# Attention before a mixture of experts: the softmax guard and the factor 8 carried by a 121st row of the matmuls

## The chip, the core and the metric

The kernel runs on one core of one Trainium2 chip, as one launch. The metric is the device time of that launch in microseconds (us). The core has five engines with a queue each: PE (TensorE, matrix products), DVE (VectorE), ACT (ScalarE), POOL (GpSimd) and SP (SyncE, which here issues transfers). An engine takes its instructions in order, so an instruction that waits holds back everything behind it on that engine. SBUF is the on-chip memory of 128 partitions, PSUM the memory that PE writes.

## The reference

```python
k_p = k.reshape(B, H, Sp, pool, D).mean(axis=3)      # B, H, S, D = 8, 8, 576, 64; pool = 8, Sp = 72
v_p = v.reshape(B, H, Sp, pool, D).mean(axis=3)
scores = scale * np.matmul(q, k_p.transpose(0, 1, 3, 2))
scores = scores - np.max(scores, axis=-1, keepdims=True)
attn = np.exp(scores)
attn = attn / (np.sum(attn, axis=-1, keepdims=True) + 1e-09)
attn_out = np.matmul(attn, v_p)
...
x = attn_out.transpose(0, 2, 1, 3).reshape(B, S, H * D)
# each token: an expert e (its best, or that of the token before, by a local gate), then
out[b, s] = p[e] * (np.maximum(x[b, s] @ w1[e], 0.0) @ w2[e])
```

The `1e-09` in the fourth line from the attention's end is the guard that this case is about. The factor 8 is the pool: the kernel sums eight values where the reference takes their mean.

## The kernel before

The attention is cut into 20 units (`units`): four pairs of batches by five, the first four of a pair with 128 partitions of queries in two columns, the fifth (`stacked`) with the last 64 queries of both batches. All eight heads of a batch have 8 x 72 = 576 keys in a row, and these are cut into five pieces of `KC` = 120 keys (`VB` holds where each begins). A piece covers parts of two or three heads; `VCH` lists them, and there are 11 such (piece, head) columns in all.

For a unit, PE makes the scores (L504, L510), DVE takes the maxima (`mx`, L525) and subtracts them (`ap`, L528), ACT takes exp (L538), PE transposes pieces of 120 keys (L554) and ACT copies them into `aT` (L401). Then PE multiplies `aT[0:120]` with `vaug` (L585). `vaug` holds for each of the 11 columns a mask times the pooled values (64 numbers), the mask itself, and 9 numbers for routing: so one product gives the output, the softmax sum and the routing numbers. ACT copies the product to `osb` (L401). `scale` then makes the reciprocal of the sums on DVE in two instructions:

```python
nc.vector.tensor_scalar(out=rr[:, 0:ns], in0=osb[:, 0:ns, HD], scalar1=EPS, scalar2=float(POOL), op0=ALU.add, op1=ALU.mult)
nc.vector.reciprocal(out=rr[:, 0:ns], in_=rr[:, 0:ns])
```

These are L602 and L603. `rr` then scales the routing numbers (`lgx`, L607) and the rows (`xs`, L623, on POOL and DVE).

The masks `mk` are made once by `mask_consts` (L204 to L220): POOL sets a table, DVE turns it into 0 and 1 in small instructions (L212 to L216) and copies it into the four `vaug` buffers (L220). `prep_k` loads keys (`kk`), DVE adds them eight by eight into `kd` (L428, one buffer) and ACT spreads that into `kdz` (L432). `prep_v` loads values, pools them into `vs` (L416 on DVE, L409 to L411 on POOL), PE transposes them (L456), ACT copies them to `vT`, and PE multiplies with the gate (L465, L468).

The order of all this is a list written out by hand: `PLAN` holds steps as `name:number`, and `do` issues them in that order on whichever engine each uses. `cm` is `mask_consts`, `cr` is `route_consts` (small constants on POOL, L223 to L251, used much later), `cz` clears a `kdz` buffer on POOL (L817), `fr` is the step with L602 and L603, `wa` are products that only keep PE at work. After `PLAN`, `PLAN_B` and `PLAN_C` begin the expert layers, which share the queues with the last units; then a loop over blocks of 256 tokens runs (from L1252).

Of the kernel before, what the change touches and what calls it, by code (L numbers as in the profile page):

```python
# [16 lines left out]
P = 128  # L17
# [90 lines left out]
def moe_attention(ctx: ExitStack, tc: tile.TileContext, q, q_st, k, v, v_st, w_gate, w1, w2, out):  # L108
# [95 lines left out]
    def mask_consts():  # L204
        nc.gpsimd.iota(prow_i, pattern=[[0, 1]], base=0, channel_multiplier=1)
        nc.vector.tensor_copy(out=prow, in_=prow_i)
        nc.vector.tensor_scalar(out=bm[:, 1:2], in0=prow, scalar1=float(HP), scalar2=None, op0=ALU.is_ge)
        nc.vector.tensor_scalar(out=bm[:, 0:1], in0=prow, scalar1=float(HP), scalar2=None, op0=ALU.is_lt)
        for c, hs in enumerate(VCH):
            for i, h in enumerate(hs):  # L210
                nc.gpsimd.memset(mkt[:, VOFF[c] + i:VOFF[c] + i + 1], float(VB[c] - G * h))
        nc.vector.tensor_scalar(out=mkt, in0=mkt, scalar1=prow[:, 0:1], scalar2=None, op0=ALU.add)  # L212
        nc.vector.tensor_scalar(out=mk, in0=mkt, scalar1=0.0, scalar2=None, op0=ALU.is_ge)
        nc.vector.tensor_scalar(out=mkt, in0=mkt, scalar1=float(G), scalar2=None, op0=ALU.is_lt)
        nc.vector.tensor_tensor(out=mk, in0=mk, in1=mkt, op=ALU.mult)
        nc.vector.scalar_tensor_tensor(out=mk[:, VOFF[4]:VOFF[4] + 1], in0=prow, scalar=float(4 * KC - VB[4]),  # L216
                                       in1=mk[:, VOFF[4]:VOFF[4] + 1], op0=ALU.is_ge, op1=ALU.mult)

        for t in vaug:
            nc.vector.tensor_copy(out=t[:, :, HD], in_=mk)  # L220

    def route_consts():
        nc.gpsimd.affine_select(out=lt, in_=ones, pattern=[[1, P]], compare_op=ALU.is_gt, fill=0.0,  # L223
# [160 lines left out]
    with ExitStack() as actx:  # L384
# [57 lines left out]
        def prep_v(bb, cc):  # L442
            vt = vaug[bb % NBUF]
            m = 2 if cc < 2 else 1
            vt_in = buffer([P, 2, D], "vt_in")
            if m == 2:
                nc.sync.dma_start(vt_in.rearrange("p c n -> p (c n)"), v[bb, cc])
            else:
                nc.sync.dma_start(vt_in[:, 0], v_st[bb])
            yield  # L450
            vs = pooled_v[bb, cc] = ap2.tile([P, 2, HD], F32, name="vs", bufs=5)
            pooled(vs[0:KC, 0:m], vt_in[0:KC, 0:m], KC, m, {"d": 2, "s": 1}.get(pick["e"], 0))
            yield
            tp = ps_t.tile([P, 512], F32, name="tp")
            busy(tp, TFILL.get((bb, cc), 0))
            nc.tensor.transpose(out=tp[0:m * HD, 0:KC], in_=vs[0:KC, 0:m].rearrange("p c d -> p (c d)"), identity=ident[0:KC, 0:KC])  # L456
            yield
            vT = ap2.tile([P, P], F32, name="vT")
            copy(vT[0:m * HD, 0:KC], tp[0:m * HD, 0:KC])
            yield  # L460
            mp = ps_r.tile([P, 512], F32, name="rt")
            busy(mp, GFILL.get((bb, cc), 0))
            if m == 2:
                w = wg[:, 0:162] if cc == 0 else wg[:, 27:207]
                nc.tensor.matmul(out=mp[0:KC, 0:54].rearrange("p (c x) -> p c x", c=2), lhsT=vT[:, 0:KC],  # L465
                                 rhs=w.rearrange("p (c x) -> p c x", c=2)[:, :, 0:27], start=True, stop=True)
            else:
                nc.tensor.matmul(out=mp[0:KC, 0:2 * GL], lhsT=vT[0:HD, 0:KC], rhs=wg[0:HD, (H - 2) * GL:H * GL], start=True, stop=True)  # L468
            yield
            for ci in range(m):  # L470
                c = 2 * cc + ci
                o, ns = VOFF[c], len(VCH[c])
                nc.vector.tensor_tensor(out=vt[0:KC, o:o + ns, HD + 1:SEG],
                                        in0=mp[0:KC, 27 * ci:27 * ci + ns * GL].rearrange("p (h e) -> p h e", e=GL),
                                        in1=mk[0:KC, o:o + ns].unsqueeze(2).broadcast_to([KC, ns, GL]), op=ALU.mult)

        def place_v(bb, cc):
            vt, vs = vaug[bb % NBUF], pooled_v[bb, cc]
            for ci in range(2 if cc < 2 else 1):
                c = 2 * cc + ci  # L480
                o, ns = VOFF[c], len(VCH[c])
                if pick["e"] == "a":
                    for i in range(o, o + ns):
                        nc.scalar.activation(out=vt[0:KC, i, 0:HD], in_=vs[0:KC, ci, :], func=AF.Copy, scale=mk[0:KC, i:i + 1])
                    continue
                (nc.vector if pick["e"] == "d" else nc.gpsimd).tensor_tensor(
                    out=vt[0:KC, o:o + ns, 0:HD], in0=vs[0:KC, ci:ci + 1, :].broadcast_to([KC, ns, HD]),
                    in1=mk[0:KC, o:o + ns].unsqueeze(2).broadcast_to([KC, ns, HD]), op=ALU.mult)

        def queries(i):  # L490
            pr, t = units[i]
# [49 lines left out]
        class Attend:  # L541
            def __init__(self, at, pr, t):
                self.at, self.pr, self.t = at, pr, t
                self.stacked = t == 4
                self.aT = ap2.tile([P, NCH, P], F32, name="aT")

            def transpose(self, c4):
                cs = list(range(4 * c4, min(4 * c4 + 4, len(VB) if self.stacked else NCH)))
# [9 lines left out]
            def values(self, g):  # L558
# [7 lines left out]
                def heads(n, r, c0, c, lo, hi, at):  # L566
                    hs = [h for h in VCH[c] if lo <= h < hi]
                    if hs:
                        at += (hs[0] - lo) * SEG
                        o = VOFF[c] + VCH[c].index(hs[0])  # L570
                        jobs.append((n, op[r, at:at + len(hs) * SEG], self.aT[0:KC, c0 + c, r],
                                     vaug[(2 * self.pr + n) % NBUF][0:KC, o:o + len(hs), :].rearrange("p s x -> p (s x)")))
                if self.stacked:
                    lo, hi = ((0, HM), (HM, H))[g]
                    for c in range(len(VB)):
# [21 lines left out]
            def scale(self, lg):  # L597
# [196 lines left out]
        def do(name, n):  # L794
# [515 lines left out]
```

## Time and profile before

| what | value |
|---|---|
| three timed runs, median (lowest to highest) | 606.49 us (604.74 to 607.5) |
| the profiled execution: its time, its span | 610.27 us, 607.8 us |
| mean granted TensorE clock in the span | 0.992 |
| instructions in the span | 14315 |

The span runs from the first to the last instruction, so 2.47 us of the profiled execution lie outside it. [...] Durations below come from this one execution.

### The profile page before, as it was taken

Reading aid. Unit: us, or ns where it says so; the run is one execution under the profiler, and the core shown is the slowest. Engines: PE = TensorE matmul, PEld = TensorE weight load, DVE = VectorE, ACT = ScalarE, POOL = GpSimd, SP = SyncE. Lnnn points to the kernel's source line nnn. Section 1 sums busy time; section 2 is a strip of 40 time slices with the busy share of each in tenths; the row PEclk is TensorE's granted clock in tenths of the full one; section 3 lists DMA queues with packets and bytes.
Section 4 is the critical chain, followed back from the end, with each engine's and each line's share of the span. In section 5 each row is a group of like instructions: output and inputs, shape, how many; then the busy total and the mean of one; then the engine's idle time right before and its main releaser. Section 6 shows DMA issues by size and latency. Waiting matters only on the chain.

```text
span 607.8 us, 14315 instructions
## 1 busy us (share of the span) xinstructions
PE 580.0 (95%) x3316; PEld 500.3 (82%) x3317; DVE 410.0 (67%) x981; ACT 318.0 (52%) x708; POOL 283.2 (47%) x527
## 2 busy tenths in 40 slices
PE   8999998898999999999999999999999999999991
PEld 7998988796877878888888888888888888888981
DVE  7999899899857424652883585798536586525680
ACT  2778777886523223442752474667344374433561
POOL 6686786777682335233143426154252333331352
PEclk9999999999999999999999999999999999999996
DMA  8998984965103764322483467496733276223223
GB/s 347 406 354 294 361 301 114 336 164 191 36 2 104 253 218 135 109 104 69 155 312 94 142 182 296 128 339 202 294 119 114 104 228 221 104 69 121 87 74 88
DMA packets 62274, 111.96 MB, mean 184 GB/s; under 512 B 13730, under 2 KB 34210, under 8 KB 62244
## 3 DMA queue, kind: packets, MB, share of 16 engines
q1 hardware_dynamic: 53732, 89.54, 44.0%
q0 software_dynamic: 8512, 22.07, 10.5%
q8 instruction: 13, 0.21, 0.1%
q14 instruction: 17, 0.14, 0.1%
HBM read 81.88 MB, written 31.80 MB: 187 GB/s over the span
## 4 chain that ended last, share of the span: by engine, by line
PE 82%; DVE 9%; POOL 2%; issue 2%; DMA 2%; ACT 1%; POOLq 0%; DVEq 0%; ACTq 0%
PE o_ps L380 35%; PE hp L353 14%; PE hp L355 7%; PE tp L353 5%; PE hp L1006 5%; PE op L585 4%; PE sp L504 3%; PE rt L353 2%; PE tp L355 2%; DVE ap L528 1%; POOL ids L728 1%; PE rt L778 1%; PE tp L554 1%; DVE mx L525 1%; PE rt L355 1%
## 5 line engine op out<-in xcount | busy, mean ns | idle before, releaser
L353 PE MATMUL hp<-x,w1h 128*128 128x512 f32 (+1 forms) x364 | 129.3, 397 | 1.4 <-DVE hs L361 1.2
L380 PE MATMUL o_ps<-w2h,ht_h 128*128 128x512 f32 x312 | 122.7, 393 | 0.1
L380 PE MATMUL o_ps<-w2l,ht_h 128*128 128x512 f32 x312 | 121.8, 390 | 1.0 <-issue 1.0
L355 PE MATMUL hp<-x,w1l 128*128 128x256 f32 (+1 forms) x364 | 101.5, 279 | 0.0
L361 DVE TENSOR_TENSOR hs<-hp,hs 128x256 f32<-128x256 f32 (+1 forms) x91 | 37.1, 415 | 78.2 <-ACT hs L360 71.2
L380 PE MATMUL o_ps<-w2h,ht_l 128*128 128x512 f32 x312 | 87.5, 390 | 0.0
L353 PEld LDWEIGHTS hp<-x,w1h 128*128 128x128 f32 x364 | 68.4, 188 | 17.8 <-DVE hs L361 1.9
L1136 POOL TENSOR_TENSOR zf<-m_e,ob 128x1 f32<-128x1 f32 x42 | 15.7, 373 | 129.7 <-ACT ob L1124 78.2
L380 PEld LDWEIGHTS o_ps<-w2h,ht_l 128*128 128x128 f32 x312 | 58.6, 188 | 13.7 <-issue 1.1
L365 ACT ACTIVATE ht_h<-hs 128x256 fp32r<-128x256 f32 (+1 forms) x136 | 56.7, 417 | 24.9 <-DVE hs L361 11.8
L355 PEld LDWEIGHTS hp<-x,w1l 128*128 128x128 f32 x364 | 68.8, 189 | 1.1 <-issue 0.2
L380 PEld LDWEIGHTS o_ps<-w2h,ht_h 128*128 128x128 f32 x312 | 58.6, 188 | 12.1
L380 PEld LDWEIGHTS o_ps<-w2l,ht_h 128*128 128x128 f32 x312 | 58.6, 188 | 11.9 <-issue 0.6
L366 DVE SCALAR_TENSOR_TENSOR ht_l<-hs,ht_h 128x256 fp32r<-128x256 f32 (+1 forms) x136 | 58.1, 430 | 10.1 <-PE hp L355 5.2
L360 ACT COPY hs<-hp 128x256 f32<-128x256 f32 (+1 forms) x91 | 33.2, 369 | 58.5 <-PE hp L355 50.9
L585 PE MATMUL op<-vaug,aT 120*128 120x148 f32 (+3 forms) x400 | 59.6, 306 | 1.7 <-ACT osb L401 1.7
L1124 ACT ACTIVATE ob<-o_ps,m_a 128x512 f32<-128x512 f32 x40 | 27.5, 686 | 55.1 <-PE o_ps L380 50.4
L585 PEld LDWEIGHTS op<-vaug,aT 120*128 120x128 f32 (+1 forms) x400 | 51.6, 179 | 4.4 <-ACT osb L401 2.5
L1137 POOL DMA_INDIRECT out<-ob,m_e x42 | 45.4, 1080 | 18.5 <-issue 17.0
L1135 POOL TENSOR_TENSOR m_e<-m_i,zi 128x1 int32<-128x1 int32 x42 | 12.1, 287 | 78.7 <-DVE m_i L321 73.0
L328 POOL DMA_INDIRECT vt_in<-x_rows,idk x40 | 40.7, 1017 | 10.6 <-issue 8.4
L728 POOL DMA_INDIRECT ids<-pm,pos x36 | 38.6, 1071 | 14.6 <-issue 6.5
(265 smaller groups left out, 1167.9 us busy)
## 6 DMA issues: line engine op xcount, KB each, us to landing
raw<-in_moe_w SPq DMA_DIRECT2D x48, 512.0 KB
xd<-vt_in SPq DMA_DIRECT2D x20, 512.0 KB
vt_in<-xd SPq DMA_DIRECT2D x80, 128.0 KB
kk<-in_k SPq DMA_DIRECT2D x16, 576.0 KB
qt<-in_q SPq DMA_DIRECT2D x16, 512.0 KB
vt_in<-in_v SPq DMA_DIRECT2D x16, 512.0 KB
x_rows<-xs SPq DMA_DIRECT2D x16, 512.0 KB
vt_in<-in_v_st SPq DMA_DIRECT2D x8, 256.0 KB
```

Of the source, the lines that this page charges most:

```text
L328: nc.gpsimd.indirect_dma_start(out=xg[:, h, :], out_offset=None, in_=x_rows[0:NT + 1], in_offset=bass.IndirectOffsetOnAxis(ap=idk[:, h:h + ...
L353: nc.tensor.matmul(out=out, lhsT=W1[0][:, kk, f * P:(f + 1) * P], rhs=both, start=(kk == 0), stop=False, skip_group_check=True)
L355: nc.tensor.matmul(out=ps[:, 0:n], lhsT=W1[1][:, kk, f * P:(f + 1) * P], rhs=xt[:, kk, 0, 0:n], start=False, stop=(kk == KD - 1), skip_gro ...
L360: nc.scalar.copy(out=hb[:, 0, :], in_=ps[:, n:2 * n])
L361: nc.vector.tensor_tensor(out=hb[:, 1, :], in0=ps[:, 0:n], in1=hb[:, 0, :], op=ALU.add)
L365: nc.scalar.activation(out=ht[0][:, f, 0:n], in_=hb, func=AF.Relu)
L366: nc.vector.scalar_tensor_tensor(out=ht[1][:, f, 0:n], in0=hb, scalar=0.0, in1=ht[0][:, f, 0:n].bitcast(F32), op0=ALU.max, op1=ALU.subtract)
L380: nc.tensor.matmul(out=to[h], lhsT=ht[i][:, kk, h * P:(h + 1) * P], rhs=W2[j][:, kk, :], start=(n == 0), stop=(n == 3 * KF - 1))
L585: nc.tensor.matmul(out=out, lhsT=lhs, rhs=rhs, start=all(x[0] != n for x in jobs[:i]), stop=all(x[0] != n for x in jobs[i + 1:]), skip_gro ...
L728: ins = nc.gpsimd.indirect_dma_start(out=ids.rearrange("t m w -> (t m) w"), out_offset=bass.IndirectOffsetOnAxis(ap=pos[:, u:u + 1], axis= ...
L1006: nc.tensor.matmul(out=hp[f], lhsT=xt[:, kk, i, 0:P], rhs=W1[j][:, kk, s], start=(n == 0), stop=(n == len(jobs) - 1))
L1137: return nc.gpsimd.indirect_dma_start(out=outv, out_offset=bass.IndirectOffsetOnAxis(ap=m_e[h][:, 0:1], axis=0), in_=ob[:, h, :], in_offse ...
```

## The change

The guard and the factor 8 move into the products. `aT` gets a 121st row of ones (partition 120), and `vaug` a 121st row that is 0 everywhere but in the column of the mask, where it holds 8 x 1e-9. The mask column itself holds 8 in place of 1. A head that appears in two pieces must get the guard once, so the columns in `TWICE` go without it. The sum that comes out of L585 is then already 8 x (sum + 1e-9), and L602 goes: `reciprocal` reads the column of `osb` itself. For the row of ones to stay, `aT` becomes two fixed buffers (`aTs`) that POOL fills once with ones on partitions 96 to 127, at the head of `cr`; the copies overwrite partitions 0 to 119. For the rows 120 to 127 of `vaug` to be 0, the values are pooled, transposed, gated and placed over 128 rows and not 120, and the masks are 0 there.

```diff
+TWICE = slice(1, VOFF[-1], 4)
...
+        nc.vector.scalar_tensor_tensor(out=mk, in0=prow.broadcast_to([P, VOFF[-1]]), scalar=float(KC), in1=mk, op0=ALU.is_lt, op1=ALU.mult)
+        nc.vector.tensor_scalar(out=guard, in0=prow, scalar1=float(KC), scalar2=POOL * EPS, op0=ALU.is_equal, op1=ALU.mult)
+        nc.vector.tensor_scalar(out=mks, in0=mk, scalar1=float(POOL), scalar2=guard[:, 0:1], op0=ALU.mult, op1=ALU.add)
+        nc.vector.tensor_scalar(out=mks[:, TWICE], in0=mk[:, TWICE], scalar1=float(POOL), scalar2=None, op0=ALU.mult)
         for t in vaug:
-            nc.vector.tensor_copy(out=t[:, :, HD], in_=mk)
+            nc.vector.tensor_copy(out=t[:, :, HD], in_=mks)
...
+        aTs = [ap1.tile([P, NCH, P], F32, name=f"aT{i}") for i in range(2)]
...
-            nc.tensor.transpose(out=tp[0:m * HD, 0:KC], in_=vs[0:KC, 0:m].rearrange("p c d -> p (c d)"), identity=ident[0:KC, 0:KC])
+            nc.tensor.transpose(out=tp[0:m * HD, 0:P], in_=vs[:, 0:m].rearrange("p c d -> p (c d)"), identity=ident)
...
-                self.aT = ap2.tile([P, NCH, P], F32, name="aT")
+                aTs.append(aTs.pop(0))
+                self.aT = aTs[0]
...
-                        jobs.append((n, op[r, at:at + len(hs) * SEG], self.aT[0:KC, c0 + c, r],
-                                     vaug[(2 * self.pr + n) % NBUF][0:KC, o:o + len(hs), :].rearrange("p s x -> p (s x)")))
+                        jobs.append((n, op[r, at:at + len(hs) * SEG], self.aT[0:KC + 1, c0 + c, r],
+                                     vaug[(2 * self.pr + n) % NBUF][0:KC + 1, o:o + len(hs), :].rearrange("p s x -> p (s x)")))
...
-                nc.vector.tensor_scalar(out=rr[:, 0:ns], in0=osb[:, 0:ns, HD], scalar1=EPS, scalar2=float(POOL), op0=ALU.add, op1=ALU.mult)
-                nc.vector.reciprocal(out=rr[:, 0:ns], in_=rr[:, 0:ns])
+                nc.vector.reciprocal(out=rr[:, 0:ns], in_=osb[:, 0:ns, HD])
...
             elif op == "cr":
+                for t in aTs:
+                    nc.gpsimd.memset(t[P - QP:P], 1.0)
                 route_consts()
```

The order of the instructions changes at three places. The line numbers of the changed kernel are up to 9 higher. On POOL, near the start of the program, the row of ones is set between the clearing of `kdz` and the constants of `cr`. Before:

```order
L211 MEMSET mkt 128x1 x11
L817 MEMSET kdz_150 128x576
L817 MEMSET kdz_151 128x576
L223 AFFINE_SELECT lt<-ones 128x128 [waits DVE_49]
L225 AFFINE_SELECT sel<-ones 2x16
```

After:

```order
L214 MEMSET mkt 128x1 x11
L827 MEMSET kdz_152 128x576
L827 MEMSET kdz_153 128x576
L824 MEMSET aT_155 32x1280 [waits Pool_49]
L824 MEMSET aT_156 32x1280
L230 AFFINE_SELECT lt<-ones 128x128 [waits DVE_49,Pool_49]
L232 AFFINE_SELECT sel<-ones 2x16
```

Two MEMSETs of 1280 numbers a partition have come in ahead of everything in `cr`, and the first waits until POOL's own MEMSET before it has ended. On DVE, in `mask_consts` and up to the first two `kd`, before:

```order
L214 TENSOR_SCALAR mkt<-mkt 128x11
L215 TENSOR_TENSOR mk<-mk,mkt 128x11
L216 SCALAR_TENSOR_TENSOR mk<-prow,mk 128x1
L220 COPY vaug_145<-mk 128x11
L220 COPY vaug_146<-mk 128x11
L220 COPY vaug_147<-mk 128x11
L220 COPY vaug_148<-mk 128x11
L428 TENSOR_REDUCE kd<-kk 128x144 x2
```

After:

```order
L217 TENSOR_SCALAR mkt<-mkt 128x11
L218 TENSOR_TENSOR mk<-mk,mkt 128x11
L219 SCALAR_TENSOR_TENSOR mk<-prow,mk 128x1
L222 SCALAR_TENSOR_TENSOR mk<-prow,mk 128x11
L223 TENSOR_SCALAR guard<-prow 128x1
L224 TENSOR_SCALAR mks<-mk,guard 128x11
L225 TENSOR_SCALAR mks<-mk 128x3
L227 COPY vaug_147<-mks 128x11
L227 COPY vaug_148<-mks 128x11
L227 COPY vaug_149<-mks 128x11
L227 COPY vaug_150<-mks 128x11
L436 TENSOR_REDUCE kd<-kk 128x144 x2
```

Four small instructions stand between the mask and its copies, and so ahead of the first `kd`. On DVE in the steps of the first units, before:

```order
L528 TENSOR_TENSOR ap<-sp,mx 128x288
L602 TENSOR_SCALAR rr<-osb 128x16
L603 RECIPROCAL rr<-rr 128x16
L473 TENSOR_TENSOR vaug_146<-rt,mk 120x2x9
L607 TENSOR_TENSOR lgx<-osb,rr 128x144
```

After:

```order
L536 TENSOR_TENSOR ap<-sp,mx 128x288
L611 RECIPROCAL rr<-osb 128x16
L481 TENSOR_TENSOR vaug_148<-rt,mk 128x2x9
L615 TENSOR_TENSOR lgx<-osb,rr 128x144
```

One instruction of each unit's pair is gone, and RECIPROCAL follows the work before it; this repeats for all 20 units.

## Rows read from the trace of the kernel before

**Rows 1.** Page: the chain that ended last, shares of the span by engine.

```profile
PE 82%; DVE 9%; POOL 2%; issue 2%; DMA 2%; ACT 1%; POOLq 0%; DVEq 0%; ACTq 0%
```

**Rows 2.** Windows by stage: length, busy us (count) by engine, clock, DMA.

```profile
23.00:62.00 39.00, 37.96 (x309) 35.82 (x308) 37.55 (x83) 30.91 (x82) 31.22 (x46) 1.00 0.92 336
62.00:95.00 33.00, 31.05 (x258) 28.69 (x257) 30.82 (x79) 24.10 (x64) 25.35 (x37) 1.00 0.90 313
134.00:156.00 22.00, 18.31 (x138) 15.27 (x136) 20.57 (x57) 12.99 (x28) 13.76 (x16) 1.00 0.46 157
200.00:600.00 400.00, 394.51 (x1981) 333.42 (x1980) 236.53 (x503) 192.10 (x388) 144.31 (x305) 1.00 0.49 164
```

**Rows 3.** Lines L602 and L603: count, ns min/median/max, first and last start.

```profile
L602 DVE TENSOR_SCALAR rr<-osb x20: 138/166/1822, 28.4 to 151.1; 128x16 f32<-128x16 f32 x16, 128x8 f32<-128x8 f32 x4
L603 DVE RECIPROCAL rr<-rr x20: 202/253/254, 28.6 to 151.3; 128x16 f32<-128x16 f32 x16, 128x8 f32<-128x8 f32 x4
```

**Rows 4.** Timeline of DVE around unit 0's sums: start us, us.

```profile
28.36 0.16 DVE L602 TENSOR_SCALAR rr<-osb 128x16 f32<-128x16 f32 x1
28.56 0.25 DVE L603 RECIPROCAL rr<-rr 128x16 f32<-128x16 f32 x1
...
28.95 1.28 DVE L607 TENSOR_TENSOR lgx<-osb,rr 128x144 f32<-128x144 f32 x1
```

**Rows 5.** Chain, in order of time: the first and last L602 from 62 to 95.

```profile
67.31 0.16 DVE rr L602
...
93.87 0.08 DVE rr L602
```

**Rows 6.** Timeline of DVE: the longest L602, and L607 two behind it.

```profile
141.53 1.82 DVE L602 TENSOR_SCALAR rr<-osb 128x16 f32<-128x16 f32 x1
...
143.56 0.24 DVE L607 TENSOR_TENSOR lgx<-osb,rr 128x144 f32<-128x144 f32 x1
```

**Rows 7.** Timeline of POOL at five places: start us, us, idle before.

```profile
2.27 1.08 POOL L817 MEMSET kdz<- 128x576 f32 x2
...
10.20 0.73 POOL L409 TENSOR_TENSOR t<-vt_in 120x256 f32<-120x256 f32 x1 [4.59 <-DMA vt_in<-in_v_st]
...
28.78 1.29 POOL L409 TENSOR_TENSOR t<-vt_in 120x512 f32<-120x512 f32 x1
...
141.26 2.05 POOL L623 TENSOR_TENSOR xs<-osb,rr 128x512 f32<-128x512 f32 x2
...
151.63 0.61 POOL L623 TENSOR_TENSOR xs<-osb,rr 128x256 f32<-128x256 f32 x1 [1.74 <-ACT osb L401]
```

**Rows 8.** Timeline of DVE from the start to the first maxima.

```profile
2.36 1.02 DVE L212 TENSOR_SCALAR mkt<-mkt,prow 128x11 f32<-128x11 f32 x1
3.42 0.21 DVE L213 TENSOR_SCALAR mk<-mkt 128x11 f32<-128x11 f32 x1
...
4.81 1.34 DVE L428 TENSOR_REDUCE kd<-kk 128x144 f32<-128x1152 f32 x1
6.91 1.35 DVE L428 TENSOR_REDUCE kd<-kk 128x144 f32<-128x1152 f32 x1 [0.76 <-ACT kdz L432]
...
9.50 1.22 DVE L416 TENSOR_REDUCE vs<-vt_in 120x128 f32<-120x1024 f32 x1 [0.58 <-DMA vt_in<-in_v]
11.81 1.42 DVE L525 TENSOR_REDUCE mx<-sp 128x12 f32<-128x864 f32 x2 [1.09 <-PE sp L504]
```

**Rows 9.** POOL's longest MEMSET, a group by form: count, busy us, mean ns.

```profile
L290 POOL MEMSET qt<- 128x1024 f32 x2 | 1.9, 956 | 0.0
```

**Rows 10.** Timeline of PE at the start: start us, us, idle before.

```profile
1.91 7.90 PE L778 MATMUL rt<-ident 128*128 128x128 f32 x42 [1.91 <-POOL ident masks.py:199]
...
11.61 0.27 PE L456 MATMUL tp<-ident,vs 120*128 120x120 f32 x1
...
13.55 1.13 PE L440 MATMUL rt<-ident 128*128 128x128 f32 x8 [0.81 <-DVE vaug L473]
```

**Rows 11.** Window near the end: columns as in rows 2.

```profile
600.00:604.00 4.00, 0.00 (x0) 0.00 (x0) 0.00 (x0) 0.00 (x0) 0.00 (x0) 0.50 0.33 65
```

More of the change, by code (lines that the diff above doesn't have):

```diff
@@ L138, in moe_attention @@
     mkt = const.tile([P, VOFF[-1]], F32, name="mkt")
+    mks = const.tile([P, VOFF[-1]], F32, name="mks")
+    guard = const.tile([P, 1], F32, name="guard")
     prow_i = const.tile([P, 1], I32, name="prow_i")
@@ L451, in prep_v @@
             vs = pooled_v[bb, cc] = ap2.tile([P, 2, HD], F32, name="vs", bufs=5)
-            pooled(vs[0:KC, 0:m], vt_in[0:KC, 0:m], KC, m, {"d": 2, "s": 1}.get(pick["e"], 0))
+            pooled(vs[:, 0:m], vt_in[:, 0:m], P, m, {"d": 2, "s": 1}.get(pick["e"], 0))
             yield
@@ L455, in prep_v @@
             busy(tp, TFILL.get((bb, cc), 0))
-            nc.tensor.transpose(out=tp[0:m * HD, 0:KC], in_=vs[0:KC, 0:m].rearrange("p c d -> p (c d)"), identity=ident[0:KC, 0:KC])
+            nc.tensor.transpose(out=tp[0:m * HD, 0:P], in_=vs[:, 0:m].rearrange("p c d -> p (c d)"), identity=ident)
             yield
             vT = ap2.tile([P, P], F32, name="vT")
-            copy(vT[0:m * HD, 0:KC], tp[0:m * HD, 0:KC])
+            copy(vT[0:m * HD, :], tp[0:m * HD, 0:P])
             yield
@@ L464, in prep_v @@
                 w = wg[:, 0:162] if cc == 0 else wg[:, 27:207]
-                nc.tensor.matmul(out=mp[0:KC, 0:54].rearrange("p (c x) -> p c x", c=2), lhsT=vT[:, 0:KC],
+                nc.tensor.matmul(out=mp[:, 0:54].rearrange("p (c x) -> p c x", c=2), lhsT=vT,
                                  rhs=w.rearrange("p (c x) -> p c x", c=2)[:, :, 0:27], start=True, stop=True)
             else:
-                nc.tensor.matmul(out=mp[0:KC, 0:2 * GL], lhsT=vT[0:HD, 0:KC], rhs=wg[0:HD, (H - 2) * GL:H * GL], start=True, stop=True)
+                nc.tensor.matmul(out=mp[:, 0:2 * GL], lhsT=vT[0:HD, :], rhs=wg[0:HD, (H - 2) * GL:H * GL], start=True, stop=True)
             yield
@@ L472, in prep_v @@
                 o, ns = VOFF[c], len(VCH[c])
-                nc.vector.tensor_tensor(out=vt[0:KC, o:o + ns, HD + 1:SEG],
-                                        in0=mp[0:KC, 27 * ci:27 * ci + ns * GL].rearrange("p (h e) -> p h e", e=GL),
-                                        in1=mk[0:KC, o:o + ns].unsqueeze(2).broadcast_to([KC, ns, GL]), op=ALU.mult)
+                nc.vector.tensor_tensor(out=vt[:, o:o + ns, HD + 1:SEG],
+                                        in0=mp[:, 27 * ci:27 * ci + ns * GL].rearrange("p (h e) -> p h e", e=GL),
+                                        in1=mk[:, o:o + ns].unsqueeze(2).broadcast_to([P, ns, GL]), op=ALU.mult)
         def place_v(bb, cc):
@@ L483, in place_v @@
                     for i in range(o, o + ns):
-                        nc.scalar.activation(out=vt[0:KC, i, 0:HD], in_=vs[0:KC, ci, :], func=AF.Copy, scale=mk[0:KC, i:i + 1])
+                        nc.scalar.activation(out=vt[:, i, 0:HD], in_=vs[:, ci, :], func=AF.Copy, scale=mk[:, i:i + 1])
                     continue
                 (nc.vector if pick["e"] == "d" else nc.gpsimd).tensor_tensor(
-                    out=vt[0:KC, o:o + ns, 0:HD], in0=vs[0:KC, ci:ci + 1, :].broadcast_to([KC, ns, HD]),
-                    in1=mk[0:KC, o:o + ns].unsqueeze(2).broadcast_to([KC, ns, HD]), op=ALU.mult)
+                    out=vt[:, o:o + ns, 0:HD], in0=vs[:, ci:ci + 1, :].broadcast_to([P, ns, HD]),
+                    in1=mk[:, o:o + ns].unsqueeze(2).broadcast_to([P, ns, HD]), op=ALU.mult)
         def queries(i):
```

## The prediction, made before the changed kernel ran

> **What bounds the kernel now.** The page's chain, the work followed back from the last instruction, comes first: 82% of the span on PE, 9% on DVE [rows 1]. Then the windows by stage say where the change can count at all. From 200 to 600 us PE is busy for 394.51 of 400 us [rows 2]; no edited line runs there, and that stretch only moves as a whole. The rest is the attention. From 23 to 62 us PE is busy for 37.96 and DVE for 37.55 of 39 us, and the chain goes over PE. From 62 to 95 us they stand at 31.05 and 30.82 of 33, and the chain goes over DVE. From 134 to 156 us DVE is busy for 20.57 of 22 us and PE for 18.31 [rows 2]. So a shorter DVE can shorten the second and third of these stretches, as far as PE's own idle time there allows: 1.95 us (33 less 31.05) and 3.69 us (22 less 18.31).
>
> **What goes away.** L602 ran 20 times, with a median of 166 ns [rows 3]. RECIPROCAL waits for it: it starts at 28.56 us where L602 started at 28.36 [rows 4], so a unit saves 0.20 us of DVE, 20 units 4.0 us. RECIPROCAL now reads the strided column of `osb` and no longer the packed `rr`; L602 read that same column of 16 numbers in 0.16 us [rows 4], so I charge nothing for the stride. In the order of the changed kernel nothing else on DVE has moved.
>
> What of the 4.0 us lies on the chain? Five of the 20 stand on it from 62 to 95 us. The chain's pieces for them reach from 0.08 us (at 93.87) to 0.16 (at 67.31) [rows 5], and with 0.02 us of handover behind each from 0.10 to 0.18: five at 0.15 make 0.75 us. From 134 to 156 us there are four. One looks like a prize: at 141.53 us L602 took 1.82 us [rows 6]. It ended at 143.35, just behind the two `xs` instructions that POOL ran from 141.26 for 2.05 us, to 143.31 [rows 7]: it was held by POOL. RECIPROCAL was never held, since its 20 durations end at 254 ns [rows 3]. But next in DVE's queue is L607, and it is held in the same way: it took 1.28 us at 28.95 while POOL ran from 28.78 for 1.29 us [rows 4, 7], and 0.24 when it was alone [rows 6]. So the hold passes on to L607. That now begins to run at 143.31 and not at 143.56, which gives back 0.25 us and not 1.8. With 0.2 us for each of the other three, less 0.1 for overlap, that is 0.75 us. In the stretch from 23 to 62 us I count nothing, since PE sets the pace there. Together **-1.5 us**; the bounds are 0 (PE takes all of it as idle time elsewhere) and -4.0.
>
> [...]
>
> **What is added at the start.** There are two things, and they add up. First, four small DVE instructions stand ahead of the `vaug` copies. Each works on what the one before made or shares its table, so I take the step of 0.20 us from rows 4 for each: 0.8 us. Second, POOL's two MEMSETs of 1280 numbers. The longest MEMSET before has 1024 and took 956 ns [rows 9]; in proportion 1.2 us each, 2.4 together. That they cover 32 partitions and not 128 may make no difference; no row shows it. POOL itself has room: it idles 4.59 us ahead of 10.20 [rows 7], and nothing waits for the constants of `cr` in that time.
>
> DVE has no such room. L212 began at 2.36 us and took 1.02, to 3.38; POOL's MEMSETs of `kdz` ran from 2.27 for 1.08 us, to 3.35 [rows 7, 8]. L213, of the same kind and size, took 0.21 [rows 8]. So a MEMSET on POOL holds such a DVE instruction to its end, over the boundary between two. In the changed kernel the MEMSETs of `aT` run right behind, from about 3.4 to 5.8 us, and L213 (or L214, should L213 slip in between) is held. It ended at 3.63 [rows 8] and will end near 5.8: 2.15 us late. With the 0.8 us the first `kd`, at 4.81 before, starts about 2.9 us late.
>
> How much reaches the end? Behind it stand the copy on ACT and the second `kd`, whose 0.76 us of waiting is for that copy and moves with it. Then DVE has two waits that can shrink: 0.58 us for a transfer at 9.50, and 1.09 for PE's scores ahead of the maxima at 11.81 [rows 8]. That is 1.67 us of slack, so the maxima come 2.9 - 1.67 = 1.2 us late. PE covers the rest of this time with its filler products, which run until 9.8 us [rows 10]. From the maxima on there is no slack: PE itself waits 0.81 us at 13.55 for the DVE instruction right behind them [rows 10]. **+1.2 us.** The lower bound is 0: if the MEMSETs do not hold DVE, 0.8 us is less than 1.67. The upper is +2.0: all of the 3.2 us added on both engines, and a further 0.5 for holds by POOL's small constants, less 1.67.
>
> **The small terms.** The values now go through PE with 128 columns in place of 120: 24 transposes of 0.27 us [rows 10] by 8/120 are 0.4 us if all of it counted, the `vT` copies on ACT are hidden by its idle time (30.91 busy of 39 us [rows 2]). Most of the transposes lie where PE waits or overlaps them; I take **+0.1**. Eight more partitions cost DVE and POOL nothing: `kd` reduces 1152 numbers on 128 partitions in 1.34 us, `vs` 1024 on 120 in 1.22 [rows 8], 1.16 and 1.19 ns a number. The product with a 121st row has no more columns. At the end of the attention `zf` now lies over `aT`, so POOL's MEMSETs of it wait for the last unit's product; behind them stands the `xs` at 151.63, which waited 1.74 us for ACT's copy of that very product [rows 7]. So this costs nothing; without that cover it would be a few tenths.
>
> The sum is -1.5 + 1.2 + 0.1 = -0.2 us. Against its own execution that makes 610.27 us 610.1; the execution was 3.8 us above the median of the three runs, and against that median of 606.49 it gives **606.3 us**. About 0.5%, 3.0 us, is what a measurement of this kernel can tell from no change.
>
> **The rivals.** *The start costs nothing.* If a MEMSET on 32 partitions is shorter, or DVE gets its turn between the two, the delay falls below 1.67 us and only -1.5 + 0.1 is left: 605.1 us. Against it speaks L212, which waited over both MEMSETs. 0.2.
>
> *PE takes back what DVE saves, and the start is paid: slower.* For it: from 62 to 95 us PE has only 1.95 us idle, and the two engines wait for each other in turn. If the 1.5 us become idle time on DVE, 1.2 + 0.1 stay: 607.8 us. It decides from where PE's remaining idle time there falls under 0.75 us. Against it: the chain names DVE there, not PE. 0.2.
>
> *All of it comes back.* If the 4.0 us are returned in full and the start is hidden: 602.5 us; with the start paid 603.8. Against it: the first six of the 20 lie before 62 us, where PE is busy for 97%. 0.08.
>
> *The clock falls at the start.* PE will stand still for about 1.2 us more, between its first and second half of the scores and again before 13.55. The first 42 fillers took 7.90 us, 0.188 each, against 1.13 for 8 later on, 0.141 [rows 10]: such a slow spell would cost some 42 x 0.047 = 2.0 us more, 608.3 us, and up to 610 if it comes twice. [...] The pause of 0.81 us at 13.55 left it alone: the clock reads 1.00 from 23 us on [rows 2]. [...] 0.05.
>
> **How the numbers follow.** The forecast has 0.47. Its own range is 605.3 to 607.3 us. The range given reaches over the first two rivals and the scatter of the three runs, 603.9 to 608.4 us, and leaves out the last two. Faster by over 0.5% (under 603.5) is the third rival and a tail of the first, 0.10; slower by over 0.5% (over 609.5) the fourth and a tail of the second, 0.07; the same 0.83.
>
> **What would show it.** In the changed kernel's profile: POOL's two MEMSETs of 1.2 us at 3.4 us; a DVE instruction of `mask_consts` held for over 1.5 us; the first `kd` at 7.7 us in place of 4.81 and the first maxima at 13.0 in place of 11.81; 20 RECIPROCALs of at most 0.26 us; L607 of the unit at 141 us long in place of L602; DVE's busy time down by some 4 us; the stretch from 62 to 156 us shorter by 1.5 us. I am wrong if the first maxima stand at 12 us or earlier, or if the time from the first maxima to the first block of the loop has not shrunk or has shrunk by 3 us.

## The result: 0.5% slower, and the profile after

The changed kernel takes 609.31 us in the median of 12 runs, the kernel before 606.45 in as many beside them: a ratio of 1.0052, with a 95% interval from 1.0033 to 1.0070. Two more sets, each on a chip of its own, gave 1.0062 (1.0028 to 1.0096) and 1.0063 (1.0016 to 1.0110). So the change costs 3 to 4 us where 0.2 us of gain were forecast. Ratios and mean clocks leave out the runs that took over 1.5% longer than the quickest of their kernel.

The profiled execution is the quickest of its 12 (607.5 us, a span of 604.9, a mean clock of 0.994), while that of before was 3.8 us above its median; these two spans can't be set against each other, and what is read below are stages. The page's chain by engine, which answers to [rows 1]:

```profile
PE 72%; DVE 3%; DMA 3%; issue 1%; ACT 0%; POOL 0%; POOLq 0%; ACTq 0%; DVEq 0%
```

The windows by stage, as in [rows 2]:

```profile
23.00:62.00 39.00, 37.62 (x304) 35.32 (x302) 36.18 (x77) 31.01 (x82) 30.83 (x46) 1.00 0.90 334
62.00:95.00 33.00, 32.47 (x269) 30.47 (x270) 30.68 (x77) 25.89 (x68) 26.91 (x38) 1.00 0.89 313
134.00:156.00 22.00, 18.05 (x135) 15.09 (x132) 20.73 (x55) 12.86 (x29) 13.73 (x16) 1.00 0.42 144
```

DVE's share of the chain has fallen, and from 62 to 95 us PE is now the fuller engine (32.47 us against DVE's 30.68). From 134 to 156 us DVE is busy for 20.73 us, more than the 20.57 of before, though four instructions there are gone; over the whole span its busy time rose from 410.0 to 411.9 us where a fall of 4 was forecast. A held instruction counts as busy, as `lgx` does for 2.99 us at 140.41 us (below). The sums themselves went as said. The line that answers to [rows 3] shows 20 RECIPROCALs, none held:

```profile
L611 DVE RECIPROCAL rr<-osb x20: 196/242/257, 29.6 to 150.4; 128x16 f32<-128x16 f32 x16, 128x8 f32<-128x8 f32 x4
```

The start on DVE, against [rows 8] and [rows 4]:

```profile
2.36 1.02 DVE L215 TENSOR_SCALAR mkt<-mkt,prow 128x11 f32<-128x11 f32 x1
3.42 1.19 DVE L216 TENSOR_SCALAR mk<-mkt 128x11 f32<-128x11 f32 x1
4.63 1.10 DVE L217 TENSOR_SCALAR mkt<-mkt 128x11 f32<-128x11 f32 x1
...
7.42 1.35 DVE L436 TENSOR_REDUCE kd<-kk 128x144 f32<-128x1152 f32 x1
9.52 1.35 DVE L436 TENSOR_REDUCE kd<-kk 128x144 f32<-128x1152 f32 x1 [0.76 <-ACT kdz L440]
...
11.45 0.17 DVE L251 SCALAR_TENSOR_TENSOR tid<-bm,tid 128x4 f32<-128x4 f32 x1
11.53 1.21 DVE L424 TENSOR_REDUCE vs<-vt_in 128x128 f32<-128x1024 f32 x1
12.88 1.42 DVE L533 TENSOR_REDUCE mx<-sp 128x12 f32<-128x864 f32 x2
```

and on POOL, against [rows 7]:

```profile
3.41 2.30 POOL L824 MEMSET aT<- 32x1280 f32 x2
...
9.99 0.73 POOL L417 TENSOR_TENSOR t<-vt_in 128x256 f32<-128x256 f32 x1 [1.83 <-DMA vt_in<-in_v_st]
```

Two instructions of the masks, each held over one MEMSET of 1.15 us, and the first `kd` 2.61 us late. On PE, two waits where [rows 10] show products without a break until 9.8 us:

```profile
9.54 1.25 PE L512 MATMUL sp<-kdz,qt 128*128 128x144 f32 x8 [0.43 <-ACT kdz L440]
11.59 1.25 PE L512 MATMUL sp<-kdz,qt 128*128 128x144 f32 x8 [0.80 <-ACT kdz L440]
```

### The profile page after: what moved, and what is told of

Read it like the earlier page. It is cut to its first block, busy times and chain, and to the rows that moved or that the text cites. A ratio compares the mean times of both kernels' runs of the same rounds, so it can differ in the third digit from the quotient of the medians.

```text
span 604.9 us, 14297 instructions
## 1 busy us (share of the span) xinstructions
PE 579.1 (96%) x3316; PEld 500.0 (83%) x3317; DVE 411.9 (68%) x965; ACT 318.5 (53%) x708; POOL 283.3 (47%) x529
## 4 chain that ended last, share of the span: by engine, by line
PE 72%; DVE 3%; DMA 3%; issue 1%; ACT 0%; POOL 0%; POOLq 0%; ACTq 0%; DVEq 0%
PE o_ps L387 34%; PE hp L360 13%; PE hp L362 7%; PE tp L360 5%; PE hp L1016 5%; PE rt L360 2%; PE tp L362 2%; PE rt L362 1%; DMA ids<-pm,pos 1%; PE tp L313 1%; DMA qt<-x_rows,idr 1%; DMA idm<-ids 1%; DVE lgx L615 1%; DVE idr L328 0%; PE op L594 0%
## 5 line engine op out<-in xcount | busy, mean ns | idle before, releaser
L594 PE MATMUL op<-vaug,aT 121*128 121x148 f32 (+3 forms) x400 | 59.6, 306 | 1.8 <-ACT osb L409 1.7
L594 PEld LDWEIGHTS op<-vaug,aT 121*128 121x128 f32 (+1 forms) x400 | 51.5, 179 | 4.5 <-ACT osb L409 2.5
L1147 POOL DMA_INDIRECT out<-ob,m_e x42 | 44.1, 1051 | 18.6 <-issue 17.1
L335 POOL DMA_INDIRECT vt_in<-x_rows,idk x40 | 39.4, 985 | 10.3 <-issue 7.8
```

Source lines behind the costliest of these rows:

```text
L335: nc.gpsimd.indirect_dma_start(out=xg[:, h, :], out_offset=None, in_=x_rows[0:NT + 1], in_offset=bass.IndirectOffsetOnAxis(ap=idk[:, h:h + ...
L594: nc.tensor.matmul(out=out, lhsT=lhs, rhs=rhs, start=all(x[0] != n for x in jobs[:i]), stop=all(x[0] != n for x in jobs[i + 1:]), skip_gro ...
L1147: return nc.gpsimd.indirect_dma_start(out=outv, out_offset=bass.IndirectOffsetOnAxis(ap=m_e[h][:, 0:1], axis=0), in_=ob[:, h, :], in_offse ...
```

## The experiments

All ratios are to runs of the kernel before on the same chip. The clock, a share of full speed, is the mean granted clock over the runs of a kernel that went into its ratio. "First maxima" is the start of the first `mx` on DVE in the profiled execution. The 146 runs of the kernel before, e1 among them, have a mean clock of 0.9905, and 13 of them 0.987 or less.

| run | kernel | ratio, 95% interval | mean clock | first maxima, us |
|---|---|---|---|---|
| e1 | before | 0.9993, 0.9964 to 1.0023 | 0.9899 | 11.46 |
| e2, e9 | after, `aT` set later | 1.0006, 0.9970 to 1.0041; 0.9984, 0.9953 to 1.0014 | 0.9882; 0.9900 | 11.40; 11.40 |
| e3 | before, more MEMSETs | 1.0011, 0.9981 to 1.0041 | 0.9901 | 12.70 |
| e4 | before without L602 | 0.9989, 0.9954 to 1.0024 | 0.9886 | 10.59 |
| e5, e16 | after | 1.0062, 1.0028 to 1.0096; 1.0063, 1.0016 to 1.0110 | 0.9875; 0.9867 | 13.67; 13.61 |
| e6 | after, `lgx` first | 1.0042, 1.0010 to 1.0075 | 0.9890 | 12.88 |
| e7 | after, fillers, three places | 1.0113, 1.0073 to 1.0153 | 0.9843 | 12.88 |
| e8 | e2 and e6 | 1.0023, 0.9988 to 1.0058 | 0.9887 | 11.67 |
| e10 | before with the new start | 1.0069, 1.0039 to 1.0100 | 0.9882 | 14.05 |
| e11 | after with L602 back | 1.0112, 1.0054 to 1.0170 | 0.9842 | 12.92 |
| e12 | after, fillers, one place | 1.0027, 0.9988 to 1.0066 | 0.9898 | 14.05 |
| e13 | after, start filled | 1.0015, 0.9971 to 1.0059 | 0.9882 | 13.94 |
| e14, e17 | e2, handover filled | 0.9961, 0.9922 to 1.0000; 0.9984, 0.9969 to 1.0000 | 0.9919; 0.9917 | 11.39; 11.66 |
| e15 | e13 and e14 | 1.0012, 0.9966 to 1.0059 | 0.9896 | 11.58 |
| e18 | before, handover filled | 0.9992, 0.9978 to 1.0006 | 0.9919 | 10.40 |

### The halves of the change: e1 to e4, e9, e10

**e1**, the kernel before again. 

> The kernel before, unchanged, once more. All theories: about 606.5 us, a ratio of 1.00 to itself. What is wanted is the granted clock and the span of each of its runs. Theory 'the clock falls at the start': its runs read 0.990 or more nearly always, since its products have only one hole of about 1 us in the start. Theories 'only later' and 'the middle': its runs read 0.988 as often as those of the changed kernel, of which half do.

The ratio to itself is 0.9993, and its clocks reach from 0.987 to 0.993. What came unlooked for: the first maxima stand at 11.46 us, and in two relatives of it, e4 and e18, at 10.59 and 10.40. In e1 and in the kernel before they wait for PE's scores, and these stand behind the filler products. The fillers took 7.90 us in [rows 10]; in e18 they took

```profile
1.91 6.36 PE L779 MATMUL rt<-ident 128*128 128x128 f32 x42 [1.91 <-POOL ident masks.py:199]
```

In windows of a us PE makes 6 or 7 of them from 3 us on, and 11 or 12 later; the step comes at about 8 us in the kernel before, between 7 and 8 in e1, between 5 and 6 in e4 and at 5 in e18. The clock column reads 1.00 all through. That the step is the clock's is an inference from e16 below, where windows of a us that read 0.50 have 6 products each, and the three us from 12 to 15 have 15.

**e2 and e9**, the MEMSETs of `aT` later.

```diff
             elif op == "cr":
+                route_consts()
                 for t in aTs:
                     nc.gpsimd.memset(t[P - QP:P], 1.0)
-                route_consts()
```

> The changed kernel with POOL's two MEMSETs of aT moved behind the constants for routing, to where POOL was idle; nothing else. The first kd should go from 7.42 us back to about 5.4, and the first maxima from 12.88 to at most 12.0. Theory 'the late start and a fall of the clock that it sets off': 606 us or below, and granted clocks of 0.990 or more. Theory 'the late start alone, with the saving of VectorE lost': 1.1 us less than the changed kernel, 608.2. Theory 'the middle' (the 121st row, the two fixed tiles, values on 128 rows): 609 us as before, with the start mended.

> The kernel of the second run once more (POOL's two MEMSETs of aT behind the constants for routing), to halve the interval. Theory 'the late start': a ratio of 1.000 to 1.002, 2 to 3 us under the changed kernel's 1.005 to 1.006. Theory 'the middle' or 'the handover alone': 1.004 or more.

Both sets are level with before, 0.5 to 0.8% under the changed kernel's three. DVE and POOL in e9:

```profile
3.42 0.21 DVE L216 TENSOR_SCALAR mk<-mkt 128x11 f32<-128x11 f32 x1
...
5.94 1.35 DVE L436 TENSOR_REDUCE kd<-kk 128x144 f32<-128x1152 f32 x1
...
11.40 1.42 DVE L533 TENSOR_REDUCE mx<-sp 128x12 f32<-128x864 f32 x2 [0.22 <-PE sp L512]
```

```profile
5.64 2.34 POOL L825 MEMSET aT<- 32x1280 f32 x2
```

The same two MEMSETs now lie beside the copies into `vaug` and the first `kd`, which takes its usual 1.35 us. The copies are held, 1.01 to 1.20 us each in place of 0.17 to 0.36 in the changed kernel, and the trace shows nothing that waits for them. The four small instructions remain, and the waits behind them cover them, as the prediction's lower bound had it. The place of two instructions on POOL is worth the whole loss.

**e3**, the hold without the rest: before with `for i in (1, 2, 1, 2): nc.gpsimd.memset(kdz[i], 0.0)` at the head of `cr`. 

> The kernel before with four more MEMSETs on POOL where the changed kernel has those of aT, on tiles that are zeroed again later: some 2.3 us of POOL's time and nothing else. DVE's instructions for the masks should be held to about 5.7 us and the first kd start about 2.1 us late; less the slack of 1.67 us the first maxima would be 0.5 us late, 12.3 us. Theory 'the late start and a fall of the clock': 608 to 610 us, with clocks of 0.988 in some runs. Theory 'the late start alone': 607.0. Theory 'the middle': 606.5 to 607.

The first maxima come at 12.70 us, 1.2 later than in e1, and the ratio is 1.0011; its interval holds such a delay and nothing at all.

**e4**, L602's half alone.

```diff
-                nc.vector.tensor_scalar(out=rr[:, 0:ns], in0=osb[:, 0:ns, HD], scalar1=EPS, scalar2=float(POOL), op0=ALU.add, op1=ALU.mult)
-                nc.vector.reciprocal(out=rr[:, 0:ns], in_=rr[:, 0:ns])
+                nc.vector.reciprocal(out=rr[:, 0:ns], in_=osb[:, 0:ns, HD])
```

> The kernel before without L602 and nothing else changed: RECIPROCAL reads osb, and the guard and the factor 8 are left out of the computation. This is what VectorE's half of the change is worth by itself. Theory 'the late start and a fall of the clock': the saving is real, 605.0 us, 1.5 less than before. Theory 'the late start alone, with the saving lost': 606.5. Theory 'the middle' says nothing of its own here: 605.0 to 606.5.

0.9989: between the two answers, and the interval holds both.

**e10**, the start alone: the kernel before with the four instructions that make `mks` and `guard` (the copies still take `mk`), and the MEMSETs of e3. 

> The kernel before with the whole start of the changed kernel and nothing else of it: the four small instructions of mask_consts on DVE (mks and guard are made and not used), and POOL's 2.3 us of MEMSETs, on the tiles kdz. First kd at about 7.4 us, first maxima at 12.9 to 13.7. Theory 'the late start': 1.2 us or more slower than before, 1.002 to 1.005. Theory 'the handover' (L602 is still there): PE waits 0.9 to 1.2 us for oh, and the ratio is that of the start's delay alone, 1.002. Theory 'the middle': 1.000 to 1.002.

1.0069, as much as the whole change or more; e9, on the same chip, has all of the change but this start and stands at 0.9984. So the start is the cause; the 121st row, the fixed tiles and the 128 rows are not needed for it. e3's first maxima lie at 12.70 us with the same MEMSETs, e10's at 14.05. Of this 1.35 us the four small instructions explain 0.66 (the first `kd` at 7.53 us and not 6.87); most of the rest is a small constant held for 1.21 us ahead of `vs`. Neither part of the start shows a loss alone: the hold without the four instructions gives 1.0011 (e3), the four without the hold give none (e2, e9).

### The handover at 140 us: e6, e8, e11

On DVE and POOL in the changed kernel, in place of [rows 6, 7]:

```profile
140.25 0.23 DVE L611 RECIPROCAL rr<-osb 128x16 f32<-128x16 f32 x1
140.41 2.99 DVE L615 TENSOR_TENSOR lgx<-osb,rr 128x144 f32<-128x144 f32 x1
...
143.77 0.26 DVE L699 TENSOR_TENSOR oh<-rt,iota 128x72 fp32r<-128x72 f32 x1
```

```profile
140.18 3.05 POOL L631 TENSOR_TENSOR xs<-osb,rr 128x512 f32<-128x512 f32 x3
```

POOL runs three `xs` in a row where it ran two. The third belongs to the unit whose RECIPROCAL stands at 140.25. Before, L602 was held until the first two had ended, so the third had to wait for its `rr` and DVE got `lgx` through in 0.24 us [rows 6, 7]. Now `rr` is there at once, and `lgx` is held over three. e4, where only L602 is gone, shows the same: `lgx` takes 2.98 us. PE then waits for `oh`, 1.80 us in the changed kernel (1.79 in e4) and 1.15 in e1 (0.92 in the kernel before and in e3):

```profile
144.20 0.28 PE L710 MATMUL rt<-oh,lt 128*128 128x80 f32 x1 [1.80 <-DVE oh L703]
```

```profile
147.62 0.28 PE L702 MATMUL rt<-oh,lt 128*128 128x80 f32 x1 [1.15 <-DVE oh L695]
```

**e6**: in `PLAN`, `fr:16 fs:17` becomes `fs:17 fr:16`. 

> The changed kernel with one pair swapped on DVE: lgx and lg of unit 17 stand ahead of the RECIPROCAL of unit 16. POOL's third xs needs that RECIPROCAL, so it can no longer follow its first two at once. Theory 'the handover': lgx is held for 2.0 us and not 2.99, oh comes 0.9 us earlier, PE's idle time ahead of the rank products is 0.9 to 1.1 us and not 1.8 to 2.0, and the kernel is some 1 us quicker than the changed one. All others: nothing changes there, and the time is that of the changed kernel.

`lgx` is held for 2.36 us, the wait ahead of the rank products falls to 1.12 us, but the third `xs` now holds the scan `cs`, and PE waits 0.77 us more between the two rank products:

```profile
143.40 1.10 DVE L704 TENSOR_TENSOR_SCAN cs<-seg,oh 128x80 fp32r<-128x80 f32 x1
```

The hold has moved again, and the ratio, 1.0042, is within the changed kernel's interval.

**e8**, e2 and e6 together. 

> The changed kernel with both: POOL's MEMSETs of aT behind the constants for routing, and lgx of unit 17 ahead of the RECIPROCAL of unit 16. Theory 'late start and handover': the two gains add up, 1.1 to 1.5 us from the start and 0.9 from the handover, so some 1.5 us quicker than before, a ratio of 0.997 to 0.998. Theory 'the middle': no quicker than the changed kernel.

1.0023; against e2 and e9 the swap brings nothing.

**e11**: a `tensor_scalar` into `rr` ahead of RECIPROCAL, whose result RECIPROCAL overwrites. 

> The changed kernel with an instruction of L602's kind put back ahead of each RECIPROCAL: it writes rr, which RECIPROCAL then writes over, so that it does no work for the result and only takes DVE's time and can be held by POOL. Theory 'the handover': PE's idle time ahead of the rank products falls back to 0.9 to 1.2 us, fewer runs lose the clock (a mean of 0.990), and the kernel is no slower than the changed one or up to 1 us quicker, 1.003 to 1.005, though it has 4 us more work on DVE. Theory 'VectorE's saving is real': 1.5 us slower than the changed kernel, 1.008.

PE's wait is 1.14 us again, as the handover theory says, yet the ratio is 1.0112. Its six runs have the lowest mean clock of all, 0.9842, and its interval overlaps the changed kernel's, so it isn't shown whether DVE's 4 us more or the clock outweigh the shorter wait. The handover is a longer wait of PE, but no run shows what it costs in time, and it is not the cause of the loss: PE waits 2.01 us for `oh` in e2 and e9, which lose nothing.

### The clock: e5, e16, e7, e12 to e15, e17, e18

**e5 and e16**, the changed kernel again. 

> The changed kernel, unchanged, once more, beside new runs of the kernel before. Theory 'the handover' (without L602 the RECIPROCAL of the unit at 140 us is no longer held, POOL's third xs follows its first two at once, and lgx is held over three of them and not two; PE waits 1.8 to 2.0 us for oh in place of 0.9 to 1.2): about 0.8 us slower than before in all, 1.1 from the start, -0.6 from 62 to 95 us, +0.3 from the handover, so a ratio of 1.001, and up to 1.004 if the clock falls there more often. Theory 'the middle': 1.005, as measured first. Theory 'one chip only': 1.000.

> The changed kernel, unchanged, a third time. All theories: 1.005 to 1.006. Theory 'the clock': a mean granted clock of 0.986 to 0.989, under that of before; in the trace, a stretch at 0.50 in the first 30 us or from 125 to 150 us in an execution that is slow, none in a quick one.

The 33 runs of its three sets have a mean clock of 0.9878, and 13 of them lie at 0.987 or less, against 13 of 146 of the kernel before; counting every run timed, 16 of 37 against 25 of 163. A share of 0.9878 in place of 0.9905 over 606 us is, as an estimate, 1.6 us of full speed lost. e16's trace shows it happen. PE from its second wait on, and the windows around it:

```profile
9.54 1.25 PE L512 MATMUL sp<-kdz,qt 128*128 128x144 f32 x8 [1.16 <-ACT kdz L440]
11.59 1.98 PE L512 MATMUL sp<-kdz,qt 128*128 128x144 f32 x8 [0.80 <-ACT kdz L440]
```

```profile
12.00:15.00 3.00, 3.00 (x15) 2.81 (x14) 2.14 (x4) 1.15 (x5) 2.76 (x6) 0.50 1.03 416
145.00:148.00 3.00, 3.00 (x14) 2.88 (x14) 2.97 (x8) 0.58 (x1) 1.56 (x1) 0.51 0.53 176
```

The fillers ended earlier here, so PE rested for 1.16 us and not 0.43, then 0.80; from 12 to 15 us the clock is at 0.50, the second half of the scores takes 1.98 us in place of 1.25, and the maxima wait for it, 13.61 in place of 12.88. Of nine traces with the late start (the changed kernel's three, e6, e7, e10 to e13) two show such a fall in the first 25 us (e12's is below), of eleven with DVE's old or nearly old start none; a second fall stands behind the handover's wait, at 145 us. That the rest sets it off is read from the order of events; no run varied it alone. DVE adds to the delay by chance: in e5, e10, e12 and e13 one of the small constants between the second `kd` and `vs` was held too; in the changed kernel these constants stand at 10.79 to 11.62 us, beside POOL's pooling, which begins at 9.99. In e5:

```profile
11.49 1.14 DVE L251 SCALAR_TENSOR_TENSOR tid<-bm,tid 128x4 f32<-128x4 f32 x1
```

**e7 and e12**, fillers: `busy(rt, 6 if pr else 0)`, then `busy(rt, 10 if pr == 2 else 0)`, ahead of the rank products. 

> The changed kernel with six filler products on PE in its idle time ahead of the rank products of the second pair; they read and write nothing that is used. Theory 'the clock falls at the handover': the runs read granted clocks of 0.990 and more in nearly all cases, in place of half of them, the trace shows no stretch at 0.50 from 140 to 150 us, and the mean time falls by 1 us or so. If the falls come elsewhere or PE's idle time doesn't set them off, the clocks spread from 0.984 to 0.994 as before.

> The changed kernel with ten filler products in one place only, PE's idle time of 1.8 us ahead of the rank products of the third pair of samples, at 142 us (the earlier run with fillers put them ahead of three pairs). Theory 'the clock falls at the handover': no stretch at 0.50 that begins between 140 and 150 us in the trace, a mean clock of 0.990 or more against 0.989 and 0.986 of the changed kernel's two sets of runs, and 1 us quicker than that. If the falls come from other idle times, clock and time stay those of the changed kernel.

Neither tested what it was made for. The fillers write the PSUM tile that DVE's `oh` still reads, and so stood behind the wait, as extra work (and a call makes two products of the trace). Their ratios lie on both sides of the changed kernel's, 1.0113 and 1.0027. In e12:

```profile
152.09 4.13 PE L448 MATMUL rt<-ident 128*128 128x128 f32 x20 [1.89 <-DVE oh L703]
```

e12's execution is useful all the same, as the second that lost the clock at the start:

```profile
15.70:22.50 6.80, 6.72 (x29) 6.48 (x30) 3.82 (x5) 1.99 (x7) 1.42 (x3) 0.50 1.03 403
```

**e13**, the start filled and DVE left late.

```diff
-        TFILL = {(0, 1): 5}
-        GFILL = {(0, 0): 2, (0, 2): 4}
+        TFILL = {(0, 0): 1, (0, 1): 5}
+        GFILL = {(0, 0): 2, (0, 2): 6}
...
+                    busy(sp[:, 0], 3 if i == 2 and (pr, t) == (0, 0) else 0)
```

> The changed kernel with six more calls of the filler product in PE's idle times of the start: three between the two halves of the first scores, one ahead of the first transpose of values, two more ahead of the second product with the gate's weights. DVE stays as late as in the changed kernel. Theory 'the clock at the start': the idle times of 0.8 and 0.6 us go, the mean granted clock rises from 0.988 towards the 0.990 of before, and 1.5 us or more come back, 1.002 to 1.004. Theory 'holds and stalls later on': nothing changes but the holes, 1.005 to 1.006.

In its trace the wait of 0.80 us is gone, one of 1.15 us ahead of it is not. The ratio, 1.0015, is close to the 1.002 to 1.004 foreseen for the clock, but its interval also holds the changed kernel's first ratio, 1.0052, and the mean clock, 0.9882, lies among those of the changed kernel's three sets (0.9867 to 0.9892). This leaves open how much of the loss is the clock at the start.

**e14 and e17**, e2 with four calls of the filler behind the products that fill the tile for `oh`, where it is in hand.

```diff
+            busy(rt, 4 if pr == 2 else 0)
```

> The kernel with POOL's MEMSETs late, and four calls of the filler product in the third pair's expert products, where their PSUM tile is in hand: PE's idle time of 1.8 to 2.0 us ahead of the rank products should shrink to about 0.9. Theory 'the clock at the handover': no stretch at 0.50 that begins between 140 and 150 us, a mean clock of 0.990 or more against 0.989 of the two sets of runs without the fillers, and 0.5 to 1 us quicker than these, a ratio of 0.998. Otherwise 0.9995 as the mean of those two.

> POOL's MEMSETs late and four calls of the filler product in the third pair's expert products, once more. Theory 'the clock': 0.996 to 0.998 as before, with most clocks at 0.990 or more. If the last result was chance: 0.999 to 1.001, as the version without the fillers.

In e14 PE's wait falls to 1.07 us:

```profile
142.57 0.28 PE L711 MATMUL rt<-oh,lt 128*128 128x80 f32 x1 [1.07 <-DVE oh L704]
```

Of the 21 runs behind their ratios none has a clock of 0.987 or less; of 34 without the fillers (e2, e8, e9) 9 do. Counting every run timed, 3 of 24 do against 11 of 36, a weaker sign. e17's own trace reads 0.50 from 141 to 144 us. The ratios, 0.9961 and 0.9984, both have intervals that end at 1.0000: e14's is the lowest of all, e17's is that of e9 without fillers, and neither is shown to be quicker than before.

**e15**, the fillers at both places. 

> POOL's MEMSETs late, and the fillers at both places. If both holes cost clock: the best of all versions, 0.997, with a mean clock of 0.990 or more. If not: 0.9995, and the fillers cost nothing or a few tenths.

1.0012: no gain.

**e18**, the kernel before with e14's fillers. 

> The kernel before with the same fillers and nothing of the change. Its idle time of PE ahead of the rank products is only 0.9 to 1.2 us. If the fillers do good wherever PE waits there: 0.998. If they matter only with the longer wait that comes without L602: 1.000 or a few tenths of a us slower.

0.9992: with L602 in place the fillers bring nothing that shows.

## Why the prediction was wrong

**The start, +1.2 us.** Its mechanism was seen: MEMSETs of 1.15 us for 1.2 forecast, the masks held (two instructions for 1.19 and 1.10 us, where one was to be held for over 1.5), the first `kd` at 7.42 us for 7.7, the maxima at 12.88 for 13.0. What failed is the subtraction of 1.67 us of slack, and with it the yardstick. 1.09 us of that slack was DVE's wait for PE's scores [rows 8], taken for a fixed property of the kernel. It belongs to an execution in which PE's pace rose late: the fillers took 7.90 us there [rows 10], and the maxima began at 11.81. In e4 and e18, where they ended sooner, the maxima wait for nothing. In four executions of kernels with the old start they began at 11.81, 11.46, 10.59 and 10.40, 11.07 in the mean; in nine with the late start at 12.88 to 14.05, 13.43 in the mean. So the term is +2.4 us and not +1.2, as far as so few executions tell. Held constants, in four of the nine, are part of it; the prediction had them only as 0.5 us in the upper bound, and not at this place.

**The clock.** This was a rival with a chance of 0.05, "608.3 us, and up to 610 if it comes twice". It happened, in some executions, at the start and again at the handover, and the mean clock puts an estimated 1.6 us on the median run. The step that failed is the reason for the low chance: a pause of 0.81 us at 13.55 that had left the clock alone [rows 10] was taken to cover two pauses in a row, one of them longer. That a rest of PE sets the clock back was the author's estimate: in the kernel before the clock reads 1.00 over that pause, from 12 to 15 us, and 0.50 only behind the last product [rows 11]. e16 lost it after pauses of 1.16 and 0.80 us. The changed kernel's own profiled execution, with pauses of 0.43 and 0.80 us, lost nothing: it reads 1.00 from 12 to 15 us.

**L602, -1.5 us.** The half from 62 to 95 us is right. From the seventh RECIPROCAL to the eleventh it takes 24.56 us in the changed kernel (68.44 to 93.00) and 25.26 in e1 (68.25 to 93.51), 0.7 less for a forecast of 0.75. In all 14 traces without L602 it takes 24.53 to 24.57, in the six with it, or with e11's stand-in, 25.02 to 26.48, 1.0 more in the mean:

```profile
68.44 0.23 DVE L611 RECIPROCAL rr<-osb 128x16 f32<-128x16 f32 x1
...
93.00 0.21 DVE L611 RECIPROCAL rr<-osb 128x16 f32<-128x16 f32 x1
```

```profile
68.25 0.25 DVE L603 RECIPROCAL rr<-rr 128x16 f32<-128x16 f32 x1
...
93.51 0.25 DVE L603 RECIPROCAL rr<-rr 128x16 f32<-128x16 f32 x1
```

The half from 134 to 156 us is wrong in sign. The hold did pass to `lgx`, as said, but grew from 1.82 to 2.99 us, since POOL's third `xs` no longer waited for a held L602: PE's wait rose by 0.65 to 0.9 us where 0.75 were to be saved. The prediction looked at who is held, and not at what POOL may do earlier once DVE is not.

**The small terms.** Transposes of 128 rows take 0.27 us as before, and the MEMSETs of `zf` at 150.05 us took 0.13 and held nothing of note; +0.1 and 0 stand. The products with a 121st row have the same median, 290 ns; over 128 rows DVE's `vs` has 1207 ns as over 120, POOL's first step of pooling 1266 for 1269.

With the terms as measured the sum is +2.4 - 0.7 + 0.8 + 0.1 = +2.6 us, and up to 1.6 for the clock, so 2.6 to 4.2 (the clock's share of the 2.4 is counted twice in the upper end). The three sets stand at 3.1 to 3.8. That they agree is no proof of the single terms: the delay of the maxima is from few executions, and the 0.8 is a wait of PE, not a time.

**What the sum leaves out.** The prediction's last sign, the time from the first maxima to the loop, can't be read from single executions: to the first product of L1006 (L1016 in the changed kernel), a line of the loop, it is 214.8 and 219.3 us in the kernel before and e1, and 210.4, 212.6 and 219.2 in the changed kernel's three. One cause of such scatter is in the traces, and no experiment was aimed at it. At 121 to 128 us an `lgx` of DVE stands close to a `w1l` of POOL. In 14 traces it is through first; in six POOL holds it for 2.93 to 3.48 us, PE then waits 2.89 to 3.04 us for `ap`, and the clock reads 0.50 at that place. In the changed kernel and in e10:

```profile
122.23 0.23 DVE L615 TENSOR_TENSOR lgx<-osb,rr 128x72 f32<-128x72 f32 x1
```

```profile
126.73 2.93 DVE L614 TENSOR_TENSOR lgx<-osb,rr 128x72 f32<-128x72 f32 x1
```

```profile
132.69 3.90 PE L511 MATMUL sp<-kdz,qt 128*128 128x144 f32 x16 [3.04 <-DVE ap L535]
```

The six spans are 612.2 to 618.8 us, the others at most 608.7 but for e16 with 614.5. Five of the six have the late start (e7, e10 to e13) and one is e1, but the changed kernel's own three traces are not among them. Whether the late start makes this hold more frequent, and how much of the loss and of the lower clock comes by it, stays open.

## What to carry to other kernels

A constant that is set once can cost more than twenty instructions that it saves: set it where the engine beside it is not waited for, here behind the DVE chain that the first scores need (1.0006 and 0.9984 there, 1.0052 to 1.0063 ahead of it). Slack counts only if it is there in several executions: the wait of 1.09 us that was counted on here was 0.87 in one other and gone in two. When an instruction that used to be held goes, ask what the holder will do next, and not only who is held in its place.

## What the runs showed of the hardware

A MEMSET on 32 partitions took 1.15 us for its 1280 numbers; in proportion to 1024 on 128 partitions, 956 ns [rows 9], it would be 1.2. DVE's small mask instructions waited for POOL's MEMSETs in some places over two in a row (L215: 1.02 us), in others over one each (L216 and L217: 1.19 and 1.10), and in e10 one instruction waited over all six (3.08 us); in e9 the reduction beside the same MEMSETs took its usual 1.35 us, while the copies into `vaug` took 1.01 to 1.20.
